# Chunks of w3 loaded two ahead and split one ahead, blocks of g loaded one a round

## The chip, the cores and the metric

The kernel runs on one core of one Trainium2 chip. The metric is the device time of the program in microseconds. Times of before and after are medians of several runs; a profile comes from one further execution.

## The reference

Sigmoid attention feeds a bilinear feed-forward block. In float32, with 8 batches, 12 heads, 448 positions, head size 64, 768 model columns and 1024 inner columns:

```python
scores = scale * np.matmul(q, k.transpose(0, 1, 3, 2)) - np.log(S)
attn = 1.0 / (1.0 + np.exp(-scores))
x = np.matmul(attn, v)                 # heads joined: 3584 tokens x 768
a = x @ w1
b = x @ w2
h = a * b @ w3                         # (a * b) @ w3
out = h @ w_out
```

The weights come as 64-bit words, which the kernel decodes on the chip to float32.

## The kernel before

The program has four stages in a row. First the attention of all batches, with the products x @ w1 and x @ w2 of the batch before filled in between; each finished g = a * b goes to DRAM (`g_dram`), and the decoded w3 goes there too (`w3_dram`), one chunk of 128 x 1024 for each of eight `ic`. Second, a stage in which the last batch's up products run on TensorE (lines around 319) while w_out is read and decoded in sixteen half rows (`raw` read on SyncE's queue, `magnitude` on ScalarE, seven instructions of `decode` and `split` on VectorE) into `woh` and `wol`, a high and a low part. Third, the w3 w_out stage: W = w3 @ w_out is computed as eight chunks of w3 times two halves of w_out. Each `product` is 24 matmuls of 128 x 384 on one PSUM bank (line 538); four banks take turns. A chunk has to be loaded (`w3`, line 454, 512 KB) and split into `w3h` (cast on ScalarE, line 67) and `w3l` (subtraction on VectorE, line 68). From the products the seven combinations A11 to S4 are formed that the last stage uses as stationary operands, in a scheme of Strassen's kind with seven products instead of eight. Fourth, the last stage: the combinations times combinations of blocks of g (line 654), seven products for each of four groups of two batches, with out stored as each is finished.

The third stage goes over `ic` from 0 to 3 and handles chunk `ic` and chunk `ic + 4` in each round. Every tile of a chunk has two buffers. Ahead of the stage the queue holds the loads of the four blocks b11, b21, b12, b22 of g for the first group (line 494, 896 KB each), and ahead of that the read, decode and up work described.

What sets the order: in the attention stage all engines but VectorE follow the program; between it and the w3 stage a scheduler orders the instructions of all engines; from `everything` on, TensorE and SyncE follow the program, while ScalarE and VectorE are ordered by the scheduler, and instructions that are ready early can move up into the w_out stage. SyncE issues its loads one by one, and one that waits holds up those behind it.

Names in the profile drop digits: `w<-w_dram` is the load of a w3 chunk, `gf<-g_dram` that of a block of g, `raw<-w_out` that of half a row block of w_out. In the order lists a number behind an underscore tells tiles apart: w_7289 is chunk 0.

Of the kernel before, what the change touches and what calls it, by code (L numbers as in the profile page):

```python
# [11 lines left out]
F32 = mybir.dt.float32  # L12
F32R = mybir.dt.float32r
U32 = mybir.dt.uint32
AF = mybir.ActivationFunctionType
ALU = mybir.AluOpType
# [9 lines left out]
def sigmoid_attention_bilinear_ffn(  # L26
# [16 lines left out]
    nc = tc.nc  # L43
# [3 lines left out]
    P = 128  # L47
# [5 lines left out]
    NF = DF // P  # L53
# [9 lines left out]
    w3_dram = dram.tile([NF, P, NF, P], F32, name="w3_dram")  # L63
    g_dram = dram.tile([NF, P, NT], F32, name="g_dram")

    def split(dst_hi, dst_lo, src, hi_engine, lo_engine):
        hi_engine(out=dst_hi, in_=src)  # L67
        lo_engine.tensor_tensor(out=dst_lo, in0=src, in1=dst_hi, op=ALU.subtract)  # L68
# [265 lines left out]
    def take(stream, n):  # L334
        for _ in range(n):
            next(stream, None)
# [111 lines left out]
    p3 = phase_w.enter_context(tc.tile_pool(name="p3", bufs=2, side="right"))  # L448
    woh = p3.tile([P, NF, DM], F32R, name="woh", bufs=1)
    wol = p3.tile([P, NF, DM], F32R, name="wol", bufs=1)  # L450

    def w3_chunk(ic):
        w3 = p3.tile([P, NF, P], F32, name="w3")
        nc.sync.dma_start(out=w3, in_=w3_dram[ic])
        w3h = p3.tile([P, NF, P], F32R, name="w3h")
        w3l = p3.tile([P, NF, P], F32R, name="w3l")
        split(w3h, w3l, w3, nc.scalar.copy, nc.vector)
        return w3h, w3l

    banks = itertools.cycle(("up", "av"))  # L460
    filler = up(B - 1, xs[B - 1], banks)
    for jc in range(NF):
        take(filler, 10)
        for half in range(2):
# [2 lines left out]
            raw = load_words(src, p3)  # L467
            f = decode(raw, magnitude(raw))
            split(woh[:, jc, ms], wol[:, jc, ms], f, nc.scalar.copy, nc.vector)
    w3s = {0: w3_chunk(0)}  # L470
    take(filler, 10 ** 6)
    phase_x.close()
    phase_d.close()

    NH = NF // 2
    NG = B // 2
    A11, A12, A22, S1, S2, S3, S4 = range(7)


    stat_h = [pw.tile([P, 4, NH, NM], F32R, name="w") for _ in range(2)]  # L480
    stat_l = [pw.tile([P, 4, NH, NM], F32R, name="w") for _ in range(2)]

    def stationary(which):
        return stat_h[which // 4][:, which % 4], stat_l[which // 4][:, which % 4]

    p4 = ctx.enter_context(tc.tile_pool(name="p4", bufs=1, side="left"))

    own = {g: {} for g in range(NG)}

    def load_block(group, name):  # L490
        j, t = {"b11": (0, 0), "b21": (1, 0), "b12": (0, 1), "b22": (1, 1)}[name]
        gf = p4.tile([P, NH, S], F32, name="gf", bufs=4)
        tokens = slice((2 * group + t) * S, (2 * group + t + 1) * S)
        nc.sync.dma_start(
            out=gf, in_=g_dram[j * NH:(j + 1) * NH, :, tokens].rearrange("f p t -> p f t")
        )
        own[group][name] = gf

    HALVES = (slice(0, NH // 2), slice(NH // 2, NH))

    def subtract_blocks(out, in0, in1):
        for fs in HALVES:
            nc.vector.tensor_tensor(out=out[:, fs], in0=in0[:, fs], in1=in1[:, fs], op=ALU.subtract)
            yield

    def split_block(dst, src):
        for fs in HALVES:
            split(dst[0][:, fs], dst[1][:, fs], src[:, fs], nc.scalar.copy, nc.vector)
            yield

    def moving(pool):
        n = 1 if pool is p4 else 2
        return (pool.tile([P, NH, S], F32R, name="gh", bufs=n),
                pool.tile([P, NH, S], F32R, name="gl", bufs=n))
# [2 lines left out]
    everything.enter_context(tc.manual_schedule(engines={ET.PE, ET.SP}))  # L517

    BLOCKS = ("b11", "b21", "b12", "b22")
    for name in BLOCKS:  # L520
        load_block(0, name)
    ready_blocks = {0: moving(p4)}
    for _ in split_block(ready_blocks[0], own[0]["b11"]):
        pass
    for _ in subtract_blocks(own[0]["b11"], own[0]["b12"], own[0]["b11"]):
        pass

    def put(which, ic, src):
        h, l = stationary(which)
        split(h[:, ic], l[:, ic], src, nc.scalar.copy, nc.vector)  # L530

    def product(ic, half):
        w3h, w3l = w3s[ic]
        ms = slice(half * NM, (half + 1) * NM)
        acc = ps.tile([P, 512], F32, name="up", tag=next(banks), bufs=2)[:, :NM]
        for jc in range(NF):
            for m, (a, w) in enumerate(((w3h, woh), (w3h, wol), (w3l, woh))):
                nc.tensor.matmul(  # L538
                    acc, a[:, jc], w[:, jc, ms],
                    start=(jc == 0 and m == 0), stop=(jc == NF - 1 and m == 2),  # L540
                )
        return acc

    def temp():
        return p3.tile([P, NM], F32, name="tw", bufs=4)

    def combination(in0, in1, op):
        t = temp()
        nc.vector.tensor_tensor(out=t, in0=in0, in1=in1, op=op)
        return t  # L550

    for ic in range(NH):
        w3s[ic + NH] = w3_chunk(ic + NH)
        a21 = temp()
        nc.scalar.copy(out=a21, in_=product(ic, 1))
        acc = product(ic, 0)
        a11 = temp()
        nc.scalar.copy(out=a11, in_=acc)
        put(A11, ic, acc)
        put(S3, ic, combination(a11, a21, ALU.subtract))  # L560
        del w3s[ic]
        if ic + 1 < NH:
            w3s[ic + 1] = w3_chunk(ic + 1)
        acc = product(ic + NH, 1)
        s1 = combination(acc, a21, ALU.add)
        put(A22, ic, acc)
        put(S1, ic, s1)
        s2 = combination(s1, a11, ALU.subtract)
        put(S2, ic, s2)
        acc = product(ic + NH, 0)  # L570
        s4 = combination(acc, s2, ALU.subtract)
        put(A12, ic, acc)
        put(S4, ic, s4)
        del w3s[ic + NH]
    phase_w.close()
    p5 = ctx.enter_context(tc.tile_pool(name="p5", bufs=1, side="right"))

# [63 lines left out]
    for n in range(7 * NG):  # L641
# [4 lines left out]
        for mc in range(MC):  # L646
# [3 lines left out]
            acc = accs[bank, mc][:, :S]  # L650
# [38 lines left out]
```

## Time and profile before

| | us |
|---|---|
| median of 3 runs | 1076.16 |
| lowest, highest run | 1073.64, 1076.51 |
| profiled execution, its time | 1073.27 |
| profiled execution, its span | 1071.2 |
| w3 w_out stage in it, first matmul to the last stage's first | 779.4 to 861.2 |

The span reaches from the first instruction to the last, and the time has some 2 us around it. Times inside the trace count from the start of the span. An idle time in square brackets stands ahead of the instruction that ended it, with what released it.

### The profile page before, as it was taken

What the parts mean: (1) busy time and instruction counts of PE and PEld (TensorE: products, weight loads), DVE (VectorE), ACT (ScalarE), POOL (GpSimd) and SP (SyncE); (2) the same over time, 40 slices, a digit from 0 to 9 for tenths busy, and PEclk for the clock granted to TensorE, in tenths of its full rate; (3) what the DMA queues carried; (4) which work ended last, traced back from release to release, by engine and by line L of the source; (5) the groups of instructions that cost most, each with busy time, mean ns of one, the idle gap of its engine ahead of it and who ended that gap; (6) DMA issues with size and microseconds to landing.
All of it is one profiled execution on the core that took longest, in us unless ns stands there. A gap on an engine that the chain in (4) does not pass through costs nothing.

```text
span 1071.2 us, 14399 instructions
## 1 busy us (share of the span) xinstructions
PE 1049.5 (98%) x5094; PEld 917.6 (86%) x5094; DVE 792.2 (74%) x1180; ACT 603.9 (56%) x861; POOL 190.6 (18%) x277
## 2 busy tenths in 40 slices
PE   8999899999999999999999999999959999999998
PEld 3256799999999899999999999999959999999997
DVE  5997878788878888878888887748864366656553
ACT  5854666776776777677667676753333242313230
POOL 0002432323233232323323233300000000000000
PEclk9999999999999999999999999999989999999999
DMA  8754334444444445444444434205462023343402
GB/s 260 232 161 140 103 109 109 122 131 116 126 118 127 106 122 137 112 126 127 118 123 124 121 109 124 62 23 160 137 211 76 21 93 108 135 133 108 138 35 78
DMA packets 102616, 129.18 MB, mean 121 GB/s; under 512 B 8144, under 2 KB 97424, under 8 KB 102544
## 3 DMA queue, kind: packets, MB, share of 16 engines
q1 hardware_dynamic: 102544, 128.25, 40.8%
q8 instruction: 41, 0.67, 0.3%
q14 instruction: 31, 0.25, 0.1%
HBM read 98.34 MB, written 29.88 MB: 120 GB/s over the span
## 4 chain that ended last, share of the span: by engine, by line
PE 81%; DVE 10%; DMA 5%; issue 2%; ACT 1%; SPq 1%; ACTq 0%; DVEq 0%
PE up L319 35%; PE up L654 19%; PE av L256 10%; PE sp L200 9%; PE up L538 6%; DMA raw<-w_out 2%; DMA raw<-w 2%; DVE f L95 2%; DVE raw L100 2%; PE sp L226 1%; DVE f L103 1%; DVE w L68 1%; DMA w<-w_dram 1%; DVE raw L99 1%; DVE raw L87 1%
## 5 line engine op out<-in xcount | busy, mean ns | idle before, releaser
L319 PE MATMUL up<-xh,w 128*128 128x448 f32 x1536 | 466.9, 367 | 0.0
L319 PEld LDWEIGHTS up<-xh,w 128*128 128x128 f32 x1536 | 288.5, 188 | 31.6 <-issue 5.3
L319 PE MATMUL up<-xl,w 128*128 128x448 f32 x768 | 281.0, 366 | 0.0
L654 PE MATMUL up<-gh,w 128*128 128x448 f32 x672 | 192.2, 367 | 0.0
L181 ACT ACTIVATE ah<-sp,bias 128x896 fp32r<-128x896 f32 x117 | 117.6, 1005 | 115.4 <-PE sp L200 112.5
L218 DVE TENSOR_TENSOR al<-sp,ah 128x896 fp32r<-128x896 f32 x117 | 127.5, 1089 | 53.5 <-ACT sp L181 52.6
L68 POOL TENSOR_TENSOR kl<-kk,kh 128x896 fp32r<-128x896 f32 x39 | 89.5, 2294 | 399.8 <-DVE kh L67 368.4
L319 PEld LDWEIGHTS up<-xl,w 128*128 128x128 f32 x768 | 144.4, 188 | 12.5
L654 PEld LDWEIGHTS up<-gh,w 128*128 128x128 f32 x672 | 126.1, 188 | 11.3
L654 PE MATMUL up<-gl,w 128*128 128x448 f32 x336 | 123.2, 367 | 0.0
L181 ACT ACTIVATE sp<-sp,bias 128x896 f32<-128x896 f32 x117 | 113.6, 971 | 0.0
L256 PE MATMUL av<-ah,vs 128*128 128x448 f32 x312 | 102.6, 369 | 3.3 <-DVE ah L240 3.3
L68 POOL TENSOR_TENSOR vs<-vv,vs 128x256 fp32r<-128x256 f32 x78 | 68.6, 890 | 104.5 <-DVE vs L67 91.5
L256 PE MATMUL av<-al,vs 128*128 128x448 f32 x234 | 86.3, 369 | 0.4 <-DVE al L218 0.4
L200 PE MATMUL sp<-qs,kh 128*128 128x448 f32 x234 | 86.4, 369 | 0.0
L200 PE MATMUL sp<-qs,kl 128*128 128x448 f32 x234 | 86.2, 369 | 0.0
L240 DVE TENSOR_TENSOR ah<-st,ah 64x448 fp32r<-64x448 f32 x78 | 59.1, 758 | 18.6 <-ACT st L181 16.5
L67 ACT CAST gh<-gf 128x896 fp32r<-128x896 f32 x40 | 35.7, 942 | 60.4 <-PE up L654 50.0
L80 ACT ACTIVATE f<-raw 128x768 f32<-128x768 f32 (+2 forms) x48 | 34.4, 718 | 59.6 <-DMA raw<-w_out 25.1
L654 PEld LDWEIGHTS up<-gl,w 128*128 128x128 f32 x336 | 63.1, 188 | 5.6
L256 PEld LDWEIGHTS av<-ah,vs 128*128 128x128 f32 x312 | 58.6, 188 | 10.2 <-DVE ah L240 3.4
L68 DVE TENSOR_TENSOR gl<-gf,gh 128x896 fp32r<-128x896 f32 x40 | 41.8, 1087 | 30.4 <-ACT gh L67 30.4
(74 smaller groups left out, 1450.7 us busy)
## 6 DMA issues: line engine op xcount, KB each, us to landing
qq<-qT SPq DMA_DIRECT2D x78, 224.0 KB, 3.8
kk<-kT SPq DMA_DIRECT2D x78, 224.0 KB, 4.4
g_dram<-g SPq DMA_DIRECT2D x64, 224.0 KB, 2.0
gf<-g_dram SPq DMA_DIRECT2D x16, 896.0 KB, 5.1
raw<-w SPq DMA_DIRECT2D x16, 768.0 KB, 5.3
out<-o_sb SPq DMA_DIRECT2D x48, 224.0 KB, 2.0
vv<-vL SPq DMA_DIRECT2D x48, 192.0 KB, 2.7
raw<-w3T SPq DMA_DIRECT2D x16, 512.0 KB, 3.9
```

Source lines behind the costliest of these rows:

```text
L67: hi_engine(out=dst_hi, in_=src)
L68: lo_engine.tensor_tensor(out=dst_lo, in0=src, in1=dst_hi, op=ALU.subtract)
L80: nc.scalar.activation(f, raw[..., 1].bitcast(F32), AF.Abs, scale=HW_SCALE)
L95: nc.vector.scalar_tensor_tensor(out=fb, in0=fb, scalar=3, in1=high, op0=ALU.logical_shift_left, op1=ALU.bitwise_xor)
L181: nc.scalar.activation(dst, src, AF.Sigmoid, bias=bias[:n], scale=scale)
L200: nc.tensor.matmul(sp[:, j], k[:, j, at:at + n], qs[:, j], start=m == 0, stop=m == 1)
L218: nc.vector.tensor_tensor(out=al, in0=sp, in1=ah, op=ALU.subtract)
L240: nc.vector.tensor_tensor(out=a[others, j], in0=t[rows], in1=a[rows, j], op=ALU.subtract)
L256: nc.tensor.matmul(accs[j][:, :S], v[:, c, j].rearrange("p u d -> p (u d)"), a[:, j], start=first and m == 0, stop=last and m == len(ops) - 1,
L319: nc.tensor.matmul(acc[:, :S], w[:, fc, kc], x, start=(kc == 0 and m == 0), stop=(kc == NK - 1 and m == 2),)
L538: nc.tensor.matmul(acc, a[:, jc], w[:, jc, ms], start=(jc == 0 and m == 0), stop=(jc == NF - 1 and m == 2),)
L654: nc.tensor.matmul(acc, w[:, fc, ms], g[:, fc], start=start and fc == 0 and m == 0, stop=fc == NH - 1 and m == 2, skip_group_check=True,)
```

## The change

Chunks are now numbered by the order of their use, 0, 4, 1, 5, 2, 6, 3, 7 (`w3_order`), and loading and splitting are apart. Two chunks are loaded and the first is split behind the w_out decode in program order; each half round then loads the chunk two ahead and splits the one ahead. Instead of four loads of blocks of g ahead of the stage there is one in each round, and the split of b11 and the subtractions b11 - b12 stand in rounds 1 and 3. S3 is formed from the PSUM bank and no longer from its copy.

```diff
-    def w3_chunk(ic):
-        w3 = p3.tile([P, NF, P], F32, name="w3")
-        nc.sync.dma_start(out=w3, in_=w3_dram[ic])
-        w3h = p3.tile([P, NF, P], F32R, name="w3h")
-        w3l = p3.tile([P, NF, P], F32R, name="w3l")
-        split(w3h, w3l, w3, nc.scalar.copy, nc.vector)
-        return w3h, w3l
+    NH = NF // 2
+    w3_order = [ic + at for ic in range(NH) for at in (0, NH)]
+    w3f, w3s = {}, {}
+
+    def load_w3(n):
+        if n < NF:
+            w3f[n] = p3.tile([P, NF, P], F32, name="w3")
+            nc.sync.dma_start(out=w3f[n], in_=w3_dram[w3_order[n]])
+
+    def split_w3(n):
+        if n < NF:
+            w3h = p3.tile([P, NF, P], F32R, name="w3h")
+            w3l = p3.tile([P, NF, P], F32R, name="w3l")
+            split(w3h, w3l, w3f.pop(n), nc.scalar.copy, nc.vector)
+            w3s[n] = w3h, w3l
...
-    w3s = {0: w3_chunk(0)}
+    load_w3(0)
+    load_w3(1)
+    split_w3(0)
     take(filler, 10 ** 6)
...
-    for name in BLOCKS:
-        load_block(0, name)
-    ready_blocks = {0: moving(p4)}
-    for _ in split_block(ready_blocks[0], own[0]["b11"]):
-        pass
-    for _ in subtract_blocks(own[0]["b11"], own[0]["b12"], own[0]["b11"]):
-        pass
+    ready_blocks = {}
...
     for ic in range(NH):
-        w3s[ic + NH] = w3_chunk(ic + NH)
+        load_w3(2 * ic + 2)
+        split_w3(2 * ic + 1)
+        load_block(0, BLOCKS[ic])
         a21 = temp()
-        nc.scalar.copy(out=a21, in_=product(ic, 1))
-        acc = product(ic, 0)
+        nc.scalar.copy(out=a21, in_=product(2 * ic, 1))
+        acc = product(2 * ic, 0)
         a11 = temp()
         nc.scalar.copy(out=a11, in_=acc)
         put(A11, ic, acc)
-        put(S3, ic, combination(a11, a21, ALU.subtract))
-        del w3s[ic]
-        if ic + 1 < NH:
-            w3s[ic + 1] = w3_chunk(ic + 1)
-        acc = product(ic + NH, 1)
+        put(S3, ic, combination(acc, a21, ALU.subtract))
+        del w3s[2 * ic]
+        load_w3(2 * ic + 3)
+        split_w3(2 * ic + 2)
+        if ic == 1:
+            ready_blocks[0] = moving(p4)
+            for _ in split_block(ready_blocks[0], own[0]["b11"]):
+                pass
+        elif ic == 3:
+            for _ in subtract_blocks(own[0]["b11"], own[0]["b12"], own[0]["b11"]):
+                pass
+        acc = product(2 * ic + 1, 1)
...
-        acc = product(ic + NH, 0)
+        acc = product(2 * ic + 1, 0)
```

On SyncE, where the w_out decode begins, chunk 0's load is w_7289. The second and third chunk in the order of use are w_7291 and w_7558:

```order
-L454 DMA w_7289<-w_dram 128x1024
+L459 DMA w_7289<-w_dram 128x1024
+L459 DMA w_7291<-w_dram 128x1024
 L75 DMA raw<-w_out 128x768
 L331 DMA g_dram<-g 128x448
+L459 DMA w_7558<-w_dram 128x1024
 L75 DMA raw<-w_out 128x768 x2
```

Two chunk loads moved up among the first reads of w_out; on ScalarE and VectorE the split of w_7291 now stands right behind the one of w_7289 and behind the first two instructions of the third half row.

On SyncE, where the w3 stage begins, this stood before (the first five rows behind the last write of g):

```order
L494 DMA gf<-g_dram 128x4x448 x4
L454 DMA w_7572<-w_dram 128x1024
L454 DMA w_7638<-w_dram 128x1024
L454 DMA w_7710<-w_dram 128x1024
L454 DMA w_7776<-w_dram 128x1024
```

and this stands there now:

```order
L503 DMA gf<-g_dram 128x4x448
L459 DMA w_7626<-w_dram 128x1024
L459 DMA w_7698<-w_dram 128x1024
L503 DMA gf<-g_dram 128x4x448
L459 DMA w_7766<-w_dram 128x1024
L459 DMA w_7844<-w_dram 128x1024
L503 DMA gf<-g_dram 128x4x448
L459 DMA w_7912<-w_dram 128x1024
L503 DMA gf<-g_dram 128x4x448
```

One block of g now stands ahead of the fourth chunk's load, and the three others between the later ones.

On VectorE, a pair of half rows of w_out in the middle of its decode stood like this before, from the end of one half to the end of the next and on:

```order
L103 TENSOR_TENSOR f<-f,raw 128x384
L87 TENSOR_SCALAR raw<-raw 128x384
L92 TENSOR_SCALAR f<-f 128x384
L68 TENSOR_TENSOR wol<-f,woh 128x384
L95 SCALAR_TENSOR_TENSOR f<-f,raw 128x384
L330 TENSOR_TENSOR g<-up,a_sb 128x448
L99 TENSOR_SCALAR raw<-f 128x384
L100 SCALAR_TENSOR_TENSOR raw<-raw 128x384
L103 TENSOR_TENSOR f<-f,raw 128x384
L87 TENSOR_SCALAR raw<-raw 128x384
```

and stands like this now:

```order
L103 TENSOR_TENSOR f<-f,raw 128x384
L68 TENSOR_TENSOR wol<-f,woh 128x384
L87 TENSOR_SCALAR raw<-raw 128x384
L92 TENSOR_SCALAR f<-f 128x384
L330 TENSOR_TENSOR g<-up,a_sb 128x448
L95 SCALAR_TENSOR_TENSOR f<-f,raw 128x384
L99 TENSOR_SCALAR raw<-f 128x384
L100 SCALAR_TENSOR_TENSOR raw<-raw 128x384
L87 TENSOR_SCALAR raw<-raw 128x384
L103 TENSOR_TENSOR f<-f,raw 128x384
```

The subtraction wol of a second half moved ahead of the next pair's first instruction (L87), and the L87 of a second half ahead of the last instruction (L103) of the first.

## Rows read from the trace of the kernel before

**Rows 1.** The head of the page: span of the profiled execution.

```profile
span 1071.2 us, 14399 instructions
```

**Rows 2.** Chain of waits, w3 stage and end: start us, us, what ends last.

```profile
788.86 10.89 DMA w<-w_dram
...
861.39 206.18 PE up L654 x1008
```

**Rows 3.** Timeline of TensorE, w3 stage: start, duration, operation [idle before, releaser].

```profile
782.94 0.34 PE L538 MATMUL up<-woh,w3l 128*128 128x384 f32 x1
785.49 0.44 PE L538 MATMUL up<-woh,w3h 128*128 128x384 f32 x1 [2.21 <-ACT woh L67]
786.08 0.44 PE L538 MATMUL up<-wol,w3h 128*128 128x384 f32 x1 [0.15 <-DVE wol L68]
...
792.11 0.34 PE L538 MATMUL up<-woh,w3l 128*128 128x384 f32 x1
800.87 0.69 PE L538 MATMUL up<-woh,w3h 128*128 128x384 f32 x1 [8.42 <-ACT w3h L67]
...
804.52 0.34 PE L538 MATMUL up<-woh,w3h 128*128 128x384 f32 x1
```

**Rows 4.** Timeline of SyncE's queue, the same columns: loads issued before the last stage.

```profile
723.47 0.49 SPq L454 DMA_DIRECT2D w<-w_dram  x1
...
733.35 3.52 SPq L75 DMA_DIRECT2D raw<-w_out  x2
...
786.46 2.35 SPq L494 DMA_DIRECT2D gf<-g_dram  x4
788.86 41.82 SPq L454 DMA_DIRECT2D w<-w_dram  x7
```

**Rows 5.** Loads of w3 chunks (`w<-w_dram`), 700 to 871: issue to landing, us.

```profile
DMA to landing us min/median/max: 3.2/3.8/10.9
```

**Rows 6.** Timeline of ScalarE: casts of w_out and of w3 chunks.

```profile
784.92 0.51 ACT L67 CAST woh<-f 128x384 fp32r<-128x384 f32 x1 [3.21 <-DVE f L103]
...
799.77 1.04 ACT L67 CAST w3h<-w 128x1024 fp32r<-128x1024 f32 x1 [3.88 <-DMA w<-w_dram]
801.03 1.05 ACT L67 CAST w3h<-w 128x1024 fp32r<-128x1024 f32 x1 [0.21 <-DMA w<-w_dram]
```

**Rows 7.** Timeline of VectorE: decoding of w_out, split of a later chunk.

```profile
731.63 1.22 DVE L68 TENSOR_TENSOR w3l<-w,w3h 128x1024 fp32r<-128x1024 f32 x1
...
735.95 0.56 DVE L103 TENSOR_TENSOR f<-f,raw 128x384 f32<-128x384 f32 x1
...
759.30 0.36 DVE L87 TENSOR_SCALAR raw<-raw 128x384 uint32<-128x384 uint32 x1 [0.52 <-ACT f L80]
...
762.30 0.56 DVE L103 TENSOR_TENSOR f<-f,raw 128x384 f32<-128x384 f32 x1
...
763.45 0.56 DVE L68 TENSOR_TENSOR wol<-f,woh 128x384 fp32r<-128x384 f32 x1
...
765.50 0.56 DVE L103 TENSOR_TENSOR f<-f,raw 128x384 f32<-128x384 f32 x1
766.62 0.37 DVE L87 TENSOR_SCALAR raw<-raw 128x384 uint32<-128x384 uint32 x1 [0.56 <-ACT f L80]
...
812.46 1.23 DVE L68 TENSOR_TENSOR w3l<-w,w3h 128x1024 fp32r<-128x1024 f32 x1 [0.40 <-ACT w3h L67]
```

**Rows 8.** Short windows: length, busy time per engine, granted clock, DMA share, GB/s.

```profile
779.00:783.00 4.00, 4.00 (x25) 3.92 (x23) 3.32 (x9) 0.96 (x2) 0.00 (x0) 1.00 0.23 85
...
787.00:791.00 4.00, 4.00 (x16) 4.00 (x15) 0.00 (x0) 0.22 (x1) 0.00 (x0) 0.57 0.86 268
...
799.00:803.00 4.00, 1.88 (x5) 1.37 (x6) 3.76 (x4) 2.10 (x2) 0.00 (x0) 0.50 0.33 132
```

**Rows 9.** Reads of w_out (`raw<-w_out`), 715 to 790: issue to landing, us.

```profile
DMA to landing us min/median/max: 3.0/3.1/5.4
```

**Rows 10.** Loads of blocks of g (`gf<-g_dram`), 780 to 1071: issue to landing, us.

```profile
DMA to landing us min/median/max: 4.7/5.1/10.5
```

More of the change, by code (lines that the diff above doesn't have):

```diff
@@ L473, in sigmoid_attention_bilinear_ffn @@
     phase_d.close()
-    NH = NF // 2
     NG = B // 2
@@ L530, in put, with product @@
         split(h[:, ic], l[:, ic], src, nc.scalar.copy, nc.vector)
-    def product(ic, half):
-        w3h, w3l = w3s[ic]
+    def product(n, half):
+        w3h, w3l = w3s[n]
         ms = slice(half * NM, (half + 1) * NM)
@@ L573, in sigmoid_attention_bilinear_ffn @@
         put(S4, ic, s4)
-        del w3s[ic + NH]
+        del w3s[2 * ic + 1]
     phase_w.close()
```

## The prediction

> **What bounds the kernel now.** I read the page's head first, then the chain of waits, the timeline of TensorE in the w3 w_out stage, the queue's there, how long loads take to land, the timelines of ScalarE and VectorE, and last the granted clock in short windows. Outside this stage there is little to win: the span is 1071.2 us [rows 1] and from 861.39 us on the chain is TensorE alone, 206.18 us of matmuls without a wait [rows 2]. Whatever ends the w3 stage earlier therefore moves the end by as much, as long as the last stage still finds its inputs.
>
> In the w3 stage TensorE waits twice. The first wait, 2.2 us, is for the last piece of w_out, and the second, 8.4 us, is for the second chunk of w3 [rows 3]. The products of chunk 0 consist of 48 matmuls, and 21 of them run as soon as the up products end; at 782.94 the last of these starts. The next one needs the last decoded piece of w_out and starts at 785.49, and steady work resumes at 786.08 [rows 3]. The last matmul of chunk 0 starts at 792.11. The next chunk's first starts only at 800.87 [rows 3]. From 804.52 to 861.39 there are 327 matmuls at 56.87 / 327 = 0.174 us each, so chunk 0 is over at 792.11 + 0.17 = 792.28, and 8.59 us pass with no work.
>
> Why chunk 4 (the second) is late stands in the queue and the chain. SyncE first issues the four blocks of g for the last stage at 786.46, and the chunk's load comes behind them at 788.86 [rows 4]. It lands 10.89 us after issue [rows 2], while the median load of a chunk takes 3.8 [rows 5]. Then comes the cast on ScalarE, 1.04 us [rows 6], and the first matmul of the chunk can start. Both waits also cost clock: in the window 787 to 791 the granted clock is 0.57 and at 799 to 803 it is 0.50, nearly the lower level of 1.2 GHz, after full speed, 1.00 at 779 to 783, before the first [rows 8].
>
> **The change part by part.**
>
> *The second wait goes.* In the new program chunk 4 is loaded right behind chunk 0, at about 724 where chunk 0's load is at 723.47 [rows 4], and it is split right behind chunk 0's split, whose subtraction was at 731.63 [rows 7]. Its two buffers are the second pair of the ring, which nobody uses then. That is some 60 us before it is needed. What goes is 8.59 us of idling, and the slow start behind it: the first nine matmuls of the chunk take 804.52 - 800.87 = 3.65 us where nine at full pace take 1.57, so 2.08 us more. Together **-10.7 us**. I see nothing else that could hold chunk 4's products: four PSUM banks alternate, so its two results use banks that chunk 0 didn't write.
>
> *The first wait stays and shifts.* Its end is set by the decoding of w_out, a chain over the read of a half row, ScalarE's magnitude, and VectorE's seven instructions, whose last but one frees the buffer for the next read. The change puts work into this chain. First, the subtraction for chunk 4 stands on VectorE before the third half's long part: +1.22 us, the duration of chunk 0's [rows 7]. Against that, the product g is now ahead of that pair, in a gap in which VectorE waits for ScalarE, 0.56 us in a typical pair [rows 7], so some 0.5 comes back: +0.7. Second, the scheduler has ordered the later pairs anew. Before, one pair takes 759.30 to 762.86 for the first half, to 766.06 for the second, and then a wait of 0.56 to 766.62, a period of 7.32 [rows 7]. Now one subtraction wol (a step of about 0.5, its row says 0.56 [rows 7]) moves behind the second half, where it waits for the cast woh, 0.51 [rows 6]; the next magnitude stands behind that cast on ScalarE. The work shrinks to 6.76 - 0.47 = 6.29, and the gap grows to 0.51 + 0.56 and some hops, about 1.1: period 7.39. Over about five such pairs that is +0.3. The reads, 3.1 us at the median [rows 9], still land before ScalarE gets to them (2.9 + 0.5 after the buffer is free), but with little to spare. Sum **+1.0 us** on the end of decoding. Bounds: nothing, if the gaps take all of it, and +3.9, if the two added chunk loads, 1.26 us each (two queued chunks were cast at 799.77 and 801.03 [rows 6]), also delay the reads issued behind them: 1.22 + 2 x 1.26 = 3.7, and 0.2 of drift.
>
> The row on which this upper bound rests is chunk 4's load of before: behind 4 x 896 KB it needed 10.89 us [rows 2], against 3.8 [rows 5]. The Trainium skill, "DMA: Bandwidth & Descriptors", section "Queues, rings and completion order", says that each DMA engine takes the descriptors of one ring in their order; the row agrees. By that rule alone every byte put ahead of a read would delay it, and the change would bring 10.7 - 3.7 = 7.0 us; by the rows it brings more. The first added load is through before the third read is issued. The second stands just ahead of the fourth, issued at 733.35 [rows 4], which then lands at 733.35 + 3.1 + 1.26 = 737.7; ScalarE could not use it sooner, since the third half ends on VectorE at 735.95 + 0.56 [rows 7] and 1.2 later now.
>
> *Clock behind the first wait.* From 786.08 to 792.28 there are 26 matmuls, which at 0.174 are 4.5 us and took 6.2. I leave these 1.7 us in, since the wait that precedes them stays and grows a little. If the clock does not fall this time, they are a gain.
>
> *The rounds.* A chunk is 48 x 0.174 = 8.35 us of TensorE. From the third chunk on, a split waits until the chunk two earlier is done, because there are two buffers of each part. It was so before: the third chunk's subtraction is at 812.46 [rows 7], 1.2 us behind the end of the chunk that held its buffer (804.52 + 39 x 0.174 = 811.3), and its products could begin only 8.35 us after 811.3, so 6 us are spare. That cover stays. The third chunk of now is even loaded ahead of the fourth read of w_out, and split once TensorE leaves chunk 0, at about 796, 5 us early. New is that a block of g is loaded in each round, between chunk loads, and that its subtraction b12 from b11 stands on VectorE ahead of the sixth chunk's split. With a start of chunk 4 at 793.3 the fourth chunk ends at 818.3 and the fifth at 826.7. The load of the block is released by the fifth chunk's split at about 809.9 + 2.4 = 812.3; if the chunk load ahead of it and the block take their medians of 3.8 and 5.1 [rows 5, 10] one after the other, it lands at 821.2, and with 2.9 us of VectorE work the sixth chunk is ready at 824.1. Spare: 2.6 us. Cost nothing, and each microsecond beyond that costs one.
>
> *The last stage.* It needs blocks b11 and b21 first; both are in SBUF by 820, some 30 us early. Its matmuls, instructions and queue are unchanged. S3 now subtracts from PSUM, which frees nothing that is waited for. Zero.
>
> **Sum.** -10.7 + 1.0 = **-9.7 us**. The profiled execution took 1073.27 us, 2.07 more than its span, so it would become 1063.6. It lies 2.9 below the median of the runs shown, 1076.16, near the lowest run, 1073.64; from the median the same step gives 1066.5. Runs of the new kernel may fall at either end, and I take 1065.2.
>
> **The rivals.**
>
> *The reads fall behind the added loads* (the upper bound above): the gain is 7.0 us and the time 1066.3 to 1069.2. For it: one read of before, among the first, took 5.4 [rows 9]. Against: only the first three reads are near the added loads.
>
> *The decoding is not delayed and the clock stays up behind the first wait*: 10.7 + 1.7 = 12.4 less, 1060.9 to 1063.8. Against: the clock fell after a wait of only 2.2 us [rows 3, 8].
>
> *The decoding slips by a pair's delay each time, and the kernel is slower.* In the new order the instruction that opens the second half stands on VectorE ahead of the one that frees the first half's buffer. A read that lands x us later than it is looked for now holds up the next read of the other buffer too, and x is lost in each of some six pairs. With 9.7 us to give back, it decides from x = 1.6, so from reads of about 4.7 us. The typical read is 3.1 and the longest took 5.4 [rows 9]. At x = 2 the time is 12 - 9.7 = 2.3 above before, 1075.6 to 1078.5.
>
> *It doesn't do what it says*: the wait for chunk 4 goes, and one for the sixth chunk takes its place, because the block of g holds VectorE. With the longest landing of a block, 10.5 instead of 5.1 [rows 10], the sixth chunk is 5.4 - 2.6 = 2.8 us late and the restart at the lower clock costs another 2 us: a gain of about 5, 1068.4 to 1071.3. For less than 0.3% it needs two such waits.
>
> **How the numbers follow.** The forecast has 0.72, the rival of the reads 0.10, that of the clock 0.08, that of the sixth chunk 0.06, slower 0.02, and two such waits, no measurable change, 0.02. The range is 1061.0 to 1069.2: it holds the forecast from the profiled execution's 1063.6 and from the median's 1066.5, each with a microsecond or so of the unknown delay, and reaches over the clock's and the reads' rivals; about 0.1 is left above. Within 0.3% is 3.2 us, about what a measurement of this kernel can tell from no change: faster 0.96, same 0.02, slower 0.02.
>
> **What will show it.** The list of waits has no wait of TensorE for w3h of 8 us; the first product of the second chunk follows the last of chunk 0 without a gap. The wait for woh stays, some 3 us, and the last wol ends at about 787. The w3 stage ends at about 851.7 instead of 861.39, followed by the same 206 us. The queue shows chunk loads between the reads near 724 and 733, and blocks of g one by one. The granted clock has one low stretch instead of two. I am wrong if the last wol ends later than 790, if TensorE waits inside the rounds near 827, or if the last stage shows waits that it did not have.

## The result and the profile after

The changed kernel takes 1065.84 us in the median of 4 runs (1064.49 to 1066.33), the kernel before 1075.95 beside it (1073.64 to 1076.51): a ratio of 0.9908, with a 95% interval of 0.9891 to 0.9925. The forecast was 1065.2. The profiled execution has a span of 1064.1 where that of before had 1071.2 [rows 1].

The list of TensorE's waits from 770 to 900 shows one row where before had two long ones (the 8.4 us for w3h are gone, the wait for woh has grown from 2.2 to 3.7; [rows 3]):

```profile
PE up L541 <- ACT woh L67: 3.7, 1, 3.7
```

The timeline of TensorE around that wait (start, duration, operation, idle time before it; the lines left out are matmuls of the same kind) answers to [rows 3]:

```profile
784.30 0.34 PE L541 MATMUL up<-woh,w3l 128*128 128x384 f32 x1
788.32 0.69 PE L541 MATMUL up<-woh,w3h 128*128 128x384 f32 x1 [3.68 <-ACT woh L67]
788.91 0.69 PE L541 MATMUL up<-wol,w3h 128*128 128x384 f32 x1
789.39 0.53 PE L541 MATMUL up<-woh,w3l 128*128 128x384 f32 x1
...
793.87 0.46 PE L541 MATMUL up<-wol,w3h 128*128 128x384 f32 x1
794.17 0.34 PE L541 MATMUL up<-woh,w3l 128*128 128x384 f32 x1
...
795.75 0.33 PE L541 MATMUL up<-woh,w3l 128*128 128x384 f32 x1
795.92 0.33 PE L541 MATMUL up<-woh,w3h 128*128 128x384 f32 x1
```

The row at 795.75 is the last of chunk 0 and the one at 795.92 the first of chunk 4: 0.17 apart, no gap where 8.59 us had been. Between 789.39 and 793.87 the matmuls step by 0.32 us instead of 0.174. The short windows say why (the column before the last two is the granted clock, [rows 8] before):

```profile
779.00:783.00 4.00, 4.00 (x23) 3.87 (x22) 3.42 (x9) 1.50 (x3) 0.00 (x0) 1.00 0.43 122
...
787.00:791.00 4.00, 2.68 (x8) 2.38 (x9) 1.24 (x3) 0.99 (x2) 0.00 (x0) 0.54 0.40 84
791.00:795.00 4.00, 4.00 (x16) 4.00 (x16) 0.10 (x1) 0.94 (x1) 0.00 (x0) 0.61 0.86 334
795.00:799.00 4.00, 4.00 (x25) 4.00 (x24) 2.99 (x4) 2.88 (x5) 0.00 (x0) 1.00 0.00 0
```

One stretch near the lower level of 1.2 GHz follows the wait, and none follows the change of chunks. The queue (SyncE's timeline, [rows 4] before) has the chunk loads between the reads and one block of g at a time:

```profile
724.63 0.96 SPq L459 DMA_DIRECT2D w<-w_dram  x2
...
734.07 0.32 SPq L459 DMA_DIRECT2D w<-w_dram  x1
...
788.93 0.38 SPq L503 DMA_DIRECT2D gf<-g_dram  x1
789.36 10.17 SPq L459 DMA_DIRECT2D w<-w_dram  x2
```

The chain of waits ends with these two rows, so the stage is over at 854.32 where before it was 861.39, and the last stage takes the same 206.18 [rows 2]:

```profile
788.32 66.01 PE up L541 x363
854.32 206.18 PE up L666 x1008
```

**A measure that leaves the executions' own offset out.** The first read of w_out is issued at 721.32 before and at 722.67 now; up to there the two programs do the same work, and a second profile of the changed kernel (e10 below) has it at 721.90, so I take these 1.35 us as a difference between executions and not as the change. I therefore count from that read to the start of the last stage: 140.07 us before, 131.65 after, 8.4 less. The table gives it for all kernels, with the start of the last cast of woh (the end of the decoding) counted from the same read, and TensorE's wait for it.

| kernel | median, us | ratio to before, 95% interval | read to last stage | read to last cast | wait for it |
|---|---|---|---|---|---|
| before | 1075.95 | | 140.1 | 63.6 | 2.2 |
| the change | 1065.84 | 0.9908 (0.9891 to 0.9925) | 131.7 | 65.1 | 3.7 |
| the change again (e10) | 1065.86 | 0.9902 (0.9889 to 0.9914) | 130.5 | 64.9 | 2.4 |
| e0 chunk 4 alone ahead | 1068.93 | 0.9929 (0.9915 to 0.9942) | 133.5 | 65.1 | 2.6 |
| e1 four blocks in round 0 | 1066.85 | 0.9912 (0.9897 to 0.9926) | 132.1 | 65.2 | 2.7 |
| e2 blocks alone spread | 1064.61 | 0.9895 (0.9876 to 0.9915) | 130.3 | 64.9 | 2.35 |
| e3 one split on GpSimd | 1067.21 | 0.9921 (0.9905 to 0.9936) | 133.8 | 68.0 | 5.5 |
| e5 halves swapped | 1061.34 | 0.9858 (0.9843 to 0.9872) | 126.4 | 65.9 | none |
| e6 spread, swapped | 1061.80 | 0.9853 (0.9834 to 0.9872) | 124.9 | 64.2 | none |
| e7 one block ahead | 1071.02 | 0.9938 (0.9921 to 0.9956) | 136.0 | 65.0 | 2.4 |
| e8 third read buffer | 1059.70 | 0.9845 (0.9829 to 0.9861) | 124.9 | 57.2 | none |
| e9 all three edits | 1059.88 | 0.9853 (0.9840 to 0.9866) | 124.9 | 57.7 | none |

The last three columns are each of one profiled execution: those of e2 (1061.30 us) and e6 (1057.64) were the fastest of their runs. They also hold a difference of 1.1 us in the pace of the up products, told in the last section. Beside e0 to e3 the kernel before took 1076.15 us, beside e5 to e8 1076.67, beside e9 and e10 1076.44.

### The profile page after: what moved, and what is told of

Same layout as the page of the kernel before. It is cut to its first block, busy times and chain, and to the rows that moved or that the text cites. A ratio compares the mean times of both kernels' runs of the same rounds, so it can differ in the third digit from the quotient of the medians.

```text
span 1064.1 us, 14402 instructions
## 1 busy us (share of the span) xinstructions
PE 1048.7 (99%) x5094; PEld 917.0 (86%) x5094; DVE 793.0 (75%) x1180; ACT 603.7 (57%) x861; POOL 190.3 (18%) x277
## 4 chain that ended last, share of the span: by engine, by line
PE 83%; DVE 6%; DMA 5%; ACT 2%; SPq 1%; issue 1%; POOL 1%; DVEq 0%; ACTq 0%; POOLq 0%
PE up L319 34%; PE up L666 19%; PE av L256 9%; PE sp L200 8%; PE up L541 6%; PE sp L197 2%; PE av L249 2%; DMA raw<-w_out 2%; PE sp L226 1%; DVE f L103 1%; DMA raw<-w 1%; DVE raw L100 1%; ACT f L80 1%; DMA raw<-w3T 1%; SPq L149 1%
```

## The experiments

The theory: chunk 4 was late because its load stood behind four blocks of g, which themselves could only be issued when the decoding was over; what remains is the first wait and its clock. The rivals: the depth of the loads and splits, or the spreading of the blocks, is what brings the gain, or the load is late for the traffic around it and not for the bytes ahead.

**e0: chunk 4's load ahead of the blocks, all else as before.**

```diff
+    w3s[NH] = w3_chunk(NH)
     for name in BLOCKS:
         load_block(0, name)
...
-        w3s[ic + NH] = w3_chunk(ic + NH)
+        if ic:
+            w3s[ic + NH] = w3_chunk(ic + NH)
```

> The kernel before, with one load and one split moved: chunk 4 is loaded ahead of the four blocks of g. Theory (the gain comes from chunk 4's load no longer standing behind the blocks): TensorE's wait of 8.4 us for w3h at chunk 4 is gone; but chunk 1's load still stands behind the four blocks, lands near 800, and its split is ready 1.5 to 2 us after chunk 4's products end, so a short wait shows there. Some 7 to 9 us faster than before. Rival 1 (it is the spreading of the blocks over the rounds that counts): no more than 2 us faster. Rival 2 (it is the depth of two chunks ahead in all rounds): half the gain, with waits in each round.

Measured: 1068.93 us. The waits of TensorE from 770 to 900:

```profile
PE up L539 <- ACT woh L67: 2.6, 1, 2.6
PE up L539 <- ACT w3h L67: 1.4, 1, 1.4
PE up L539 <- DVE w3l L68: 1.0, 1, 1.0
```

The 8.4 us are gone with this one edit. The two short waits, for w3h at 806.64 and for w3l at 808.22, are those of the third chunk, which now is the one behind four blocks. That is the part of the gain that this kernel lacks.

**e1: the change, but with all four blocks loaded in round 0, behind chunk 4's split.**

```diff
-        load_block(0, BLOCKS[ic])
+        if ic == 0:
+            for name in BLOCKS:
+                load_block(0, name)
```

> The changed kernel, with all four blocks of g loaded in the first round, behind the third chunk's load and ahead of the fourth's. Theory: the same as the changed kernel within 1 us, some 9 to 10 us faster than before, since the first three chunks are in SBUF before the blocks are loaded and the fourth, landing near 800, is not split before its buffers come free at about 802. Rival 1 (spreading of the blocks): most of the gain lost, under 4 us faster than before.

Measured: 1066.85 us, one wait, 2.7 us for woh. With the third chunk loaded ahead of the decoding's end, too, no product waits for what stands behind the blocks, and the interval overlaps that of the change. Spreading the blocks is not needed if the loads are two ahead.

**e2: the kernel before, with only the blocks spread over the rounds.**

```diff
-    for name in BLOCKS:
-        load_block(0, name)
...
     for ic in range(NH):
         w3s[ic + NH] = w3_chunk(ic + NH)
+        load_block(0, BLOCKS[ic])
...
```

> The kernel before, with only the blocks of g spread over the rounds; chunks are still loaded and split one ahead and in one step. Here too chunk 4's load is no longer behind the blocks and stands right behind chunk 0's in the queue. Theory: the wait at chunk 4 is gone and the gain is that of the changed kernel, 9 to 10 us, with no wait in the rounds. Rival 2 (depth of two chunks ahead): waits of 2 us or more at some of the six later chunks, under 6 us faster than before.

(The split of b11 and the subtraction of b12 move into the rounds too, as in the change.) Measured: 1064.61 us, as fast as the change. The queue shows why no second edit was needed: once no block stands ahead of it, chunk 4's load moves up right behind chunk 0's.

```profile
720.66 1.67 SPq L454 DMA_DIRECT2D w<-w_dram  x2
```

So loading two ahead is one way to get chunk 4 past the blocks, and moving the blocks is another; the two together bring no more than either, within what the intervals can tell.

**e7: the kernel before, with one block instead of four ahead of chunk 4's load.**

```diff
-    for name in BLOCKS:
-        load_block(0, name)
+    load_block(0, BLOCKS[0])
...
         w3s[ic + NH] = w3_chunk(ic + NH)
+        if ic == 0:
+            for name in BLOCKS[1:]:
+                load_block(0, name)
...
```

> The kernel before, with one block of g instead of four ahead of chunk 4's load in the queue, and the three others behind it. The load can still be issued only behind the decoding. If what made it late is the bytes ahead of it, each block is worth (10.89 - 3.8) / 4 = 1.8 us: it lands some 5.6 us after its issue at about 787, is cast by 793.7, and the second wait is about 1.5 us instead of 8.4; with some 2 us of restart left in, a gain of 7, 1069. The rival, that the load is late because it shares the engines with all blocks that are in flight, wherever they stand, leaves the landing near 11 us and the time near 1076. If even the wait's remainder costs no clock, 1067.

(The subtraction of b12 moves behind them too.) Measured: 1071.02 us. The timeline of SyncE and the landing of the load that is issued at 789.93, then the timeline of ScalarE and the list of waits:

```profile
789.50 0.38 SPq L494 DMA_DIRECT2D gf<-g_dram  x1
789.93 0.50 SPq L454 DMA_DIRECT2D w<-w_dram  x1
790.47 2.02 SPq L494 DMA_DIRECT2D gf<-g_dram  x3
```
```profile
DMA to landing us min/median/max: 5.8/5.8/5.8
```
```profile
794.51 1.78 ACT L67 CAST gh<-gf 128x896 fp32r<-128x896 f32 x2 [3.87 <-DMA gf<-g_dram]
796.20 1.04 ACT L67 CAST w3h<-w 128x1024 fp32r<-128x1024 f32 x1
```
```profile
PE up L535 <- ACT woh L67: 2.4, 1, 2.4
PE up L535 <- ACT w3h L67: 2.1, 1, 2.1
PE up L535 <- DVE w3l L68: 1.1, 2, 0.9
```

With one block ahead the chunk lands 5.8 us after its issue (5.6 was expected), against 10.89 us with four [rows 2]. Three blocks that follow it did not hold it, so the rival of the traffic around it falls: the bytes ahead are the cause. The Trainium skill ("DMA: Bandwidth & Descriptors", "Queues, rings and completion order") says that each DMA engine takes the descriptors of one ring in their order; with these two landings the traces agree. The gain is 5.65 us and not the 7 expected, since the chunk's waits came to 3.0 us and not 1.5. About 0.5 us of that is ScalarE: the chunk had landed at 795.7, but its cast queued behind b11's until 796.20. Another 0.9 is the wait for w3l, the subtraction that follows the cast. I had counted neither.

**e3: the change, with chunk 4's subtraction on GpSimd.** This was to take the 1.22 us out of VectorE's decoding.

```diff
-            split(w3h, w3l, w3f.pop(n), nc.scalar.copy, nc.vector)
+            split(w3h, w3l, w3f.pop(n), nc.scalar.copy, nc.gpsimd if n == 1 else nc.vector)
```

> The changed kernel, with the subtraction for the second chunk (1.22 us on VectorE in the w_out stage) given to GpSimd, which is idle there. Theory (the decoding slips by the subtraction at its start and by its new order): the end of decoding, counted from the end of the up products, comes 0.5 to 1.2 us earlier than in the changed kernel; 10 to 11.5 us faster than before. Rival (it slips by the added loads ahead of the reads): no change in the end of decoding.

Measured: 1067.21 us, and the decoding ends 3 us later, not earlier. The timelines of GpSimd and of VectorE:

```profile
732.15 3.41 POOL L68 TENSOR_TENSOR w3l<-w,w3h 128x1024 fp32r<-128x1024 f32 x1 [36.98 <-ACT w3h L67]
```
```profile
732.09 1.22 DVE L68 TENSOR_TENSOR w3l<-w,w3h 128x1024 fp32r<-128x1024 f32 x1
733.22 2.75 DVE L103 TENSOR_TENSOR f<-f,raw 128x384 f32<-128x384 f32 x1
735.90 0.35 DVE L87 TENSOR_SCALAR raw<-raw 128x384 uint32<-128x384 uint32 x1
```

The addition in line 103 takes 2.75 us where every other one of its size takes some 0.56 [rows 7]. It reads nothing that GpSimd writes, and it ends 0.4 us behind GpSimd's instruction. So 2.2 us are lost to save 1.22. Counted from the first read, the fourth cast of woh is 2.0 behind the change (22.5 and 20.5): by these rows 1.0 of it is this. The other 1.0 comes with a new order that the scheduler made at the entry, whose part was not shown by itself. The last 0.9 came with a read that took 4.64 us near the end.

**e5: the change, with the two half products of chunk 0 in the other order.**

```diff
+        acc = product(2 * ic, 0) if ic == 0 else None
         nc.scalar.copy(out=a21, in_=product(2 * ic, 1))
-        acc = product(2 * ic, 0)
+        acc = acc or product(2 * ic, 0)
```

> The changed kernel, with the two half products of chunk 0 in the other order: the half whose last columns of w_out are decoded one step earlier runs first, so 24 matmuls (4.2 us) are put ahead of the ones that wait. The theory says that what is left of the stage's loss is the wait of 3.7 us for the last decoded piece and some 2.9 us of low clock behind it; 24 + 21 matmuls at 0.174 cover 7.8 us from the end of the up products, and the last piece is ready 8.0 us behind it, so nearly all of both should go: about 6 us below the changed kernel, 1060, with at most 1 us given back at the sixth chunk. The rival, that the low clock there does not come from the wait, gives 3.5 us, 1062.5; if the stage's pace is set by the splits of the chunks, nothing, 1065.8.

Measured: 1061.34 us, by the ratios some 5 us below the change (0.9858 and 0.9908). The decoding ends no earlier (65.9 us), but TensorE has 24 other matmuls ahead of the ones that need its last piece: the list of waits is empty, and the granted clock is 1.00 in each window from 779 to 811. That the low clock goes with the wait is thereby shown. Of the expected loss in the rounds there is a stall of 0.3 us, at 800.15, where the split of the third chunk comes a little late. I had expected 6, from a profile with a wait of 3.7, one of the longer ones (2.4 in e10).

**e6: the edits of e2 and e5 together.**

> The kernel before with only the blocks of g spread over the rounds (the earlier run that gave 1064.6), and the halves of chunk 0 swapped as well. That run's profile had a wait of 2.35 us and 1.8 us of low clock behind it, so the theory gives 1064.6 - 4.2 = 1060.4. If the old order of decoding is no better than the new one, it equals the other run with swapped halves to within 1 us; if two chunks ahead is worth something of its own in the rounds, it is 1 us or more behind that one.

Measured: 1061.80 us, the same as e5 within the intervals; being two chunks ahead has no measurable worth of its own in the rounds. (The 1.5 us between the two in the table are the pace of the up products, 1.1, and the stall of e5.)

**e8: the change with a third buffer for the reads of w_out.**

```diff
-            raw = pool.tile([P, *src.shape[1:-1], 2], U32, name="raw")
+            raw = pool.tile([P, *src.shape[1:-1], 2], U32, name="raw", bufs=3)
...
-            w3f[n] = p3.tile([P, NF, P], F32, name="w3")
+            w3f[n] = p3.tile([P, NF, P], F32, name="w3", bufs=1)
```

> The changed kernel with three buffers instead of two for the read half rows of w_out, paid for in memory by one buffer instead of two for the chunks of w3 as loaded (a chunk's load then waits for the split before). The theory of the slip: the period of a pair, 7.4 us, is the round trip of one buffer (a read of 3.1 to 3.5, 0.6 on ScalarE, 3.6 on VectorE until the buffer is free), not VectorE's work of 6.8. With a third buffer the period falls to about 6.8, the decoding ends some 4 us earlier, and TensorE's first wait and its low clock go: about 1059.5. The rival, that VectorE and its exchange with ScalarE set the period, gives less than 1 us, 1065. If one buffer for loaded chunks makes the chunks in the rounds late, slower than the changed kernel.

The edit also takes one of the two buffers of the loaded chunks, to make room, so the two early splits stand elsewhere in the decoding. Measured: 1059.70 us. Casts of woh on ScalarE, each other one of the decoding:

```profile
750.16 0.52 ACT L67 CAST woh<-f 128x384 fp32r<-128x384 f32 x1 [0.91 <-DVE f L103]
...
756.44 0.51 ACT L67 CAST woh<-f 128x384 fp32r<-128x384 f32 x1 [0.91 <-DVE f L103]
...
762.31 0.51 ACT L67 CAST woh<-f 128x384 fp32r<-128x384 f32 x1 [0.49 <-DVE f L103]
...
768.59 0.52 ACT L67 CAST woh<-f 128x384 fp32r<-128x384 f32 x1 [0.51 <-DVE f L103]
```

A pair takes 18.43 / 3 = 6.1 us instead of 7.4, and the decoding ends 7.9 us earlier than in the change (6.8 and some 4 were expected). VectorE's timeline lists no idle time from 732 to 775, so its own instructions set the pace now, and in their new order, two half rows interleaved, they take less than the 6.8 that I had added up. The end of the decoding no longer matters: its last cast starts 0.9 ahead of the stage's first product. The chain shows what is left of the stage:

```profile
719.08 63.30 PE up L319 x312
782.38 66.59 PE up L541 x384
848.97 206.18 PE up L666 x1008
```

384 matmuls in 66.59 us are 0.1734 each, with nothing between them. This is the floor of the stage as it is written.

**e9: the kernel before with the edits of e2, e5 and e8.**

> The kernel before with three single edits: blocks of g spread over the rounds, halves of chunk 0 swapped, three buffers for reads of w_out (one for chunks as loaded). Each of the two latter alone already left TensorE no wait in the stage and 66.6 us from its first product to its last, which is 384 matmuls at 0.173; so together they can bring nothing more in the stage: equal to the better of the two within what the measurement can tell, 1059 to 1062. If slow reads still cost something in some of the runs of either, the spread of the runs gets narrower, and the median lies at the lower end. The rival, that the end of decoding also sets something in the last stage, gives below 1058.

Measured: 1059.88 us, as expected no better than e8: the same floor. Its runs spread as far as those of e8 (1058.96 to 1062.05), so what moves them by 3 us is not the end of the decoding.

**e10: the changed kernel once more.**

> The changed kernel once more, for a second profile of the same program. The theory of the slip (a read that lands late passes to the end of decoding, as the round trip of a read buffer sets the pace) says that the end of decoding, taken from the issue of the first read of w_out, differs from the other profile's 65.1 us by what its slow reads differ, up to 1.5 us, and that TensorE's wait follows it one for one; the time again within 0.3% of 1065.8. The rival, that the slip is fixed by the order of the instructions, gives 65.1 again to within 0.2.

Measured: 1065.86 us. The decoding ends at 64.9 instead of 65.1, which is what the rival said. Two like profiles do not settle it, though. The start of the slip does belong to the program: the fourth cast of woh comes 20.3 to 21.2 us behind the first read in the change, e10, e0, e1, e2, e5 and e6, all with both splits at the entry, and 19.4 and 19.2 in before and e7, which have one. The end moves by as much from one execution to the next: 65.9 in e5, which has the change's decoding, and 65.0 in e7, which has that of before (63.6). The wait is 2.4 and not 3.7 for another reason, told in the last section.

## Why the prediction was right, and where it was off

**The second wait goes: -10.7.** Right, with its mechanism: no idle time and no second low stretch of clock at the change of chunks. e0 shows that moving this one load past the blocks takes the 8.4 us away, e2 that spreading the blocks alone brings the whole gain, and e7 that the bytes ahead made the load late. What the change does beyond that has no measured effect of its own (e1, e2, e6).

**The end of decoding: +1.0 forecast, +1.5 measured** (63.6 to 65.1, and 64.9 in e10). This is the term that was mis-sized. At the entry I had +1.22 for the subtraction and -0.5 for g, which would fill a gap. The casts of woh, counted from the first read, come 0.8 later for the third half row (16.5 instead of 15.7) and 1.1 later for the fourth (20.5 instead of 19.4): the 1.22 came, the 0.5 hardly did. The rows show VectorE with the two splits in a row:

```profile
732.83 1.22 DVE L68 TENSOR_TENSOR w3l<-w,w3h 128x1024 fp32r<-128x1024 f32 x1
...
735.01 1.22 DVE L68 TENSOR_TENSOR w3l<-w,w3h 128x1024 fp32r<-128x1024 f32 x1
736.15 0.55 DVE L68 TENSOR_TENSOR wol<-f,woh 128x384 fp32r<-128x384 f32 x1
...
742.87 0.37 DVE L87 TENSOR_SCALAR raw<-raw 128x384 uint32<-128x384 uint32 x1 [0.42 <-ACT f L80]
```

The gap only moved one half row on, to 742.87. The step that failed is the belief that time saved in a gap of VectorE comes back. The pace is the round trip of a read buffer, which is refilled only when VectorE is done with it. The chain of waits in the change shows one:

```profile
753.38 3.11 DMA raw<-w_out
...
756.57 0.57 ACT f L80
...
757.16 0.36 DVE raw L87
...
760.22 0.57 DVE f L103
...
760.80 3.07 DMA raw<-w_out
```

That is a read of 3.1 us, 0.6 on ScalarE and 3.6 on VectorE, 7.42 in all, and two buffers take turns, so a pair of half rows takes as long. e8, with one buffer more and the same work, brings the period from 7.4 to 6.1. What VectorE loses at the entry is therefore passed on to the end, and what it saves in a gap is waited away. e7, which has nothing of chunk 4 in the decoding, follows the kernel before to within 0.4 us over 13 of the 16 casts, and then loses 1.4 us to one read of 5.03 us, 1.0 of which is left at the end: a late read goes to the end as well. So of the 1.5 about 1 us is the entry, and the rest is within what executions differ by. The new pair order was rightly small: from the fourth half row to the last the slip grew by 0.4, forecast was 0.3.

**Clock behind the first wait: 1.7 left in.** The low stretch came as said; its price differs between executions. Counted as in the forecast, from the second matmul behind the wait (788.91), 854.32 - 788.91 = 65.41 us pass to the last stage for 362 matmuls, which at 0.1734 are 62.8: 2.6 us, 0.9 more than forecast. In e10 it is 64.45 us for 362, so 1.7.

**The rounds and the last stage: zero.** Right. The block of g lands just behind VectorE's need, and the sixth chunk's split follows it:

```profile
820.72 1.09 DVE L512 TENSOR_TENSOR gf<-gf 128x896 f32<-128x896 f32 x1 [1.21 <-DMA gf<-g_dram]
821.73 0.55 DVE L552 TENSOR_TENSOR tw<-up,tw 128x384 f32<-128x384 f32 x1
822.20 1.21 DVE L68 TENSOR_TENSOR w3l<-w,w3h 128x1024 fp32r<-128x1024 f32 x1
```

It is ready at 823.4, forecast was 824.1; TensorE comes to it at 795.92 + 4 x 8.32 = 829.2, so 5.8 us are spare, more than the 2.6 forecast because the stage started later. (The subtraction at 812.46 that the forecast calls the third chunk's is the fourth's; the 6 us worked out from it are right for the fourth.)

**The sum.** By the two profiles 8.4 us, by the second profile of the change 9.6, by the medians 10.1 and 10.6; forecast 9.7. The two terms that were too small, 0.5 for the decoding and 0.9 for the clock, turn -9.7 into -8.3 and so close the sum of the first profile; the second has the clock's price as forecast. The stage was to end at about 851.7 and ended at 854.32: 1.35 of that is the executions' offset and 1.3, in the main, these two terms. That the median lies within 0.7 us of the forecast is in part luck: 1065.2 was chosen between 1063.6 and 1066.5, and executions of one program differ by more than that.

**The rivals.** Reads behind the added loads would have cost 3.7 us at the end of decoding, and it was 1.5. The read right behind an added load, issued at 734.54, did land 4.1 us later instead of some 3.1, but the chain of waits runs over VectorE then, as the forecast had it. The clock did fall. The slip grew by 0.4 over six pairs and not by a pair's delay each time. No chunk in the rounds waited.

## What to carry to other kernels

A load that stands behind bulk transfers in one queue is best moved past them; it needs neither more depth nor more buffers, and either of the two may be moved. Where a wait of TensorE is for the last piece of a chain, put products ahead of it that don't need that piece: swapping two products brought some 5 us here, with the chain as late as before. And before sharing out an engine's work, ask whether the engine or the round trip of a buffer sets the pace: a third buffer made the decoding 7.9 us shorter, where the one attempt to relieve VectorE, e3, made it longer.

## What the runs showed of the hardware

**GpSimd holds up VectorE.** The 2.75 us in e3 are not alone. In the changed kernel's attention stage, rows of GpSimd and VectorE:

```profile
99.16 2.63 POOL L68 TENSOR_TENSOR kl<-kk,kh 128x896 fp32r<-128x896 f32 x1 [98.72 <-PE sp L197]
```
```profile
99.72 0.62 DVE L330 TENSOR_TENSOR g<-up,a_sb 128x448 f32<-128x448 f32 x1
100.25 2.35 DVE L103 TENSOR_TENSOR f<-f,raw 128x768 f32<-128x768 f32 x1
```

The addition of two tiles in SBUF (1.04 us in the mean at this size) is held and ends 0.8 us behind GpSimd's instruction, and g, which has one operand in PSUM, is not. The Trainium skill, "SBUF — State Buffer", section "SBUF: two separate sides" (under "Who interferes with whom"), says that the two engines share a pair of ports, which the one that starts first keeps for its whole instruction, also against a VectorE operation with two inputs in SBUF. Both places agree. In e3 VectorE's own subtraction started first, at 732.09, and took its usual 1.22.

**Up products come in two paces.** From the first read of w_out to the first product of the w3 stage it is 58.1 us in five of the profiles (before, after, e6, e8, e9) and 59.3 in the other seven, with the same instructions and a granted clock of 1.00: the 448-column matmuls step by 0.203 or by 0.207. The w3 stage's own do not differ. That is why the change waits 3.7 us in one profile and 2.4 in the other with the decoding over at the same point: TensorE came 1.1 us later. What sets the pace was not tried and stays open.
